# K scores of a one-query attention backward: 16 wide matmuls per head and a 32x32 transpose in place of 64 narrow ones

## The chip, the cores and the metric

The kernel runs on one core of one Trainium2 chip. A core has a matrix engine (TensorE, PE in the profile, which writes its results to a memory called PSUM), a vector engine (VectorE, DVE), a scalar engine (ScalarE, ACT), GpSimd (POOL) and a sync engine (SP) that mostly starts transfers; 16 DMA engines move data between the main memory and the on-chip memory (SBUF, 128 partitions). The metric is the time of one execution on the device in microseconds.

## What is computed

Attention with one query per head, forward and backward: 32 heads, 8192 keys of 128 numbers each, bf16. The outputs are the attention's result and the gradients of q, k and v.

```python
B, H, Sq, Skv, Dh = 1, 32, 1, 8192, 128

def _fwd_reference(q, k, v):
    scale = q.shape[-1] ** -0.5
    scores = jnp.einsum('bhqd,bhkd->bhqk', q, k) * scale
    attn = _softmax(scores, axis=-1)
    return jnp.einsum('bhqk,bhkd->bhqd', attn, v)

def reference(q, k, v, grad_out):
    _out, _vjp = jax.vjp(_fwd_reference, q, k, v)
    return (_out, *_vjp(grad_out))
```

Per head, with p the softmax of the scores s: out = sum of p v; dp = v · grad_out; ds = p (dp - sum of p dp) times the scale; dq = sum of ds k; dk = ds times q, for every key; dv = p times grad_out, for every key. K and V are read once (134 MB), dk and dv written once (134 MB). With one query, each product with K or V is a matrix times a vector, and dk and dv are outer products.

## The kernel before

A head's K, V, dk and dv are tiles of 128 partitions by 64 rows ("slots") by 128 numbers, 2 MB each: partition p holds the keys 64p to 64p + 63. All tiles of a head are processed whole; the loop over heads (line 307) overlaps two of them. In iteration h it does the first half of head h (K scores, softmax, V's part, dv) and the second half of head h - 1, called p_ in the code (the sum of p dp, ds, dk, dq). The order in which instructions are written is the order in which every engine gets them (`manual_schedule`, line 98); each engine works off its own in order and waits where data is missing.

**K scores.** The 128 numbers of a key lie along a partition, but a matmul sums over partitions, so K must be turned. `k_blocks(h, u)` (line 152) does that for a quarter u of the slots (16 of 64): one VectorE transpose of 32x32 blocks, two bf16 numbers taken as one f32 word, from Kt into the quarter u of XK, a tile with one buffer whose quarters are interleaved in memory. After it, partition 32a + j of XK holds word j of the keys of the partitions 32a to 32a + 31. `k_scores(h)` (line 161) then runs 64 matmuls with K as the stationary operand (128 columns) and `q_blk[:, h, c, :]` as the moving one: 4 columns, q's numbers in one quadrant of 32 partitions and zeros elsewhere. The 64 are 16 slots times 4 (2 word blocks times the 2 halves of a word). The scores come out in PSUM tile `s` with the quarter u in the wrong place: `s_mask` (line 171, VectorE) multiplies by `in_quad` and spreads, and `s_swap` (line 179) does 8 passes of small matmuls with `lane` that put the scores in natural rows, `x["sn"]`, partition p with its 64 keys.

**Softmax.** The maximum over the row (`mx`, L339) and over partitions (a TensorE transpose and `nbias`, L350), the exponent on ScalarE from `x["sn"]` (`e`, L355), its sum by a matmul with ones (L356), the reciprocal (`rinv`, L366), p repeated four times (`p_rep`, L368, ScalarE).

**V's part.** `v_transposes` (L198, 32 f32 transposes on TensorE per head, four to a PSUM bank), `v_copy` (L189, ScalarE, PSUM to XV), `v_scores` (L208, 16 matmuls of 512 columns, four of them side by side on quarters of the array) and in the next iteration `v_back` (L215, a VectorE transpose of the PSUM bank; L218). `pd_sum` (L280) sums p dp over partitions on TensorE, `ds_of` (L283: `pdt`, `ds`, `ds_rep`) follows on VectorE. `contract` (L232) makes out and dq in 16 matmuls of 512 columns each.

**Outer products.** `outer(h, which, r)` (L250) makes a quarter of dk or dv on VectorE and starts the store after the last quarter (the first and last head: after every second). dk and dv have two buffers each, K three, V two. The loads `load_k(h+2)` and `load_v(h+2)` and all stores are issued by SP's queue, in the order of the code.

**Row broadcast.** `rows_bc(h)` (line 269), at the head's start, brings q and grad_out of the head to all partitions by one matmul (into columns 256 to 511 of the PSUM tile `s`) and a ScalarE cast to `x["qd"]`; both outer products read it. Every 8 heads `gather_copy` and `gather` (lines 237, 241) take out and dq from their accumulators.

**Prologue.** Two small loads of q (SP's queue) and grad_out (ScalarE's queue) into `rows`, the first loads of K and V, memsets on GpSimd (`do_win`, four `win_...`), `four` (line 117, VectorE copies, L120) and four TensorE transposes that give `q_blk`.

Of the kernel before, what the change touches and what calls it, by code (L numbers as in the profile page):

```python
# [8 lines left out]
ACT = mybir.ActivationFunctionType  # L9
ALU = mybir.AluOpType  # L10
AX = mybir.AxisListType
BF16 = mybir.dt.bfloat16
F32 = mybir.dt.float32
PSUM = bass.MemoryType.PSUM

CH = 16
# [9 lines left out]
def kernel(  # L26
# [37 lines left out]

    NG = NT // 4
    NX = NT // 2
    Kt, Vt, XK, XV, st, acc = {}, {}, {}, {}, {}, {}

    def rows_of(x, h, c, parts):
        L = NT // parts  # L70
# [14 lines left out]
        nc.sync.dma_start(Vt[h][:], rows_of(v, h, 0, 1))  # L85

    rows = consts.tile([H, 2, D], BF16)
    nc.sync.dma_start(rows[:, 0, :], q.rearrange("b h s d -> (b h s) d"))
    nc.scalar.dma_start(rows[:, 1, :], grad_out.rearrange("b h s d -> (b h s) d"))
    load_k(0)  # L90
    load_v(0)
# [14 lines left out]
    for which in ("p", "ds"):  # L106
        wins[which] = []
        for i in range(2):
            w = consts.tile([P, NG, 2 * QD - 4], BF16, name=f"win_{which}{i}")
            nc.gpsimd.memset(w[:], 0.0)  # L110
            wins[which].append(w)
    in_quad = consts.tile([P, NQ], F32)
    nc.vector.reduce_sum(in_quad[:], ident[:].rearrange("p (a i) -> p a i", a=NQ), axis=AX.X)

# [37 lines left out]
    def k_blocks(h, u):  # L152


        if u == 0:
            XK[h] = ktpool.tile([P, CH, NB, NCH, QD], F32, tag="XK", name="XK_sb")
        nc.vector.transpose(XK[h][:, :, :, u, :],  # L157
                            slots(Kt[h], u, NCH).rearrange("p g d -> p (g d)").bitcast(F32).rearrange(
                                "p (g w j) -> p g w j", g=CH, w=NB))

    def k_scores(h):
        x = st[h]
        out = x["s"][:, 0:NT].rearrange("p (a g) -> p g a", a=NQ)
        cols = XK.pop(h).rearrange("p g w u i -> p (g w u i)").bitcast(BF16).rearrange(
            "p (g w ui e) -> p g w e ui", g=CH, w=NB, e=2)
        for g in range(CH):
            for c in range(2 * NB):
                nc.tensor.matmul(out[:, g, :], lhsT=cols[:, g, c // 2, c % 2], rhs=q_blk[:, h, c, :],  # L168
                                 start=(c == 0), stop=(c == 2 * NB - 1), skip_group_check=True)

    def s_mask(h):
        x = st[h]
        x["sm"] = small.tile([P, NQ, NCH, CH], F32, tag="sm", name="sm")
        nc.vector.tensor_tensor(  # L174
            x["sm"][:], x["s"][:, 0:NT].rearrange("p (a g) -> p a g", a=NQ).unsqueeze(2)
            .to_broadcast([P, NQ, NCH, CH]),
            in_quad[:].unsqueeze(1).unsqueeze(3).to_broadcast([P, NQ, NCH, CH]), op=ALU.mult)

    def s_swap(h):

        x = st[h]
        x["sn"] = x["s"][:, 128:128 + NT]
        for a in range(NQ):
            nc.tensor.matmul(x["s"][a * QD:(a + 1) * QD, 128:128 + NT], lhsT=lane[:],  # L184
                             rhs=x["sm"][:, a].rearrange("p u g -> p (u g)"),
                             start=True, stop=True, skip_group_check=True)

    def v_copy(h, c):
        nc.scalar.copy(XV[h][:, c * TB:(c + 1) * TB, :], st[h].pop(("T", c))[:])  # L189
# [60 lines left out]
    def outer(h, which, r):  # L250
        x = st[h]
        if r == 0:
            x[which] = gpool.tile([P, NT, D], BF16, tag=which, name="G_" + which)
        G, dst = x[which], out_2 if which == "dk" else out_3
        rep, row = x["ds"] if which == "dk" else x["p"], x["qd"][:, 0 if which == "dk" else 1, :]
        Q = NT // 4
        nc.vector.tensor_tensor(  # L257
            slots(G, r, 4).rearrange("p n (a b) -> p n a b", b=R),
            slots(rep, r, 4).unsqueeze(2).to_broadcast([P, Q, D // R, R]),
            row.rearrange("p (a b) -> p a b", b=R).unsqueeze(1).to_broadcast([P, Q, D // R, R]),  # L260
            op=ALU.mult)
        parts = 1
        if h == 0 or h == H - 1:
            parts = 2
        if r % (4 // parts) == 4 // parts - 1:
            c = r // (4 // parts)
            nc.sync.dma_start(rows_of(dst, h, c, parts), slots(G, c, parts))

    def rows_bc(h):
        x = st[h]  # L270
        x["s"] = psS.tile([P, 512], F32, tag="s", name="s_ps")
        nc.tensor.matmul(x["s"][:, 256:512], lhsT=ident[0:H, h:h + 1].to_broadcast([H, P]),  # L272
                         rhs=rows[:].rearrange("h a d -> h (a d)"), start=True, stop=True,
                         skip_group_check=True)
        x["qd"] = small.tile([P, 2, D], BF16, tag="qd", name="qd")
        nc.scalar.copy(x["qd"][:].rearrange("p a d -> p (a d)"), x["s"][:, 256:512])  # L276

    def pd_sum(h):
        x = st[h]
# [27 lines left out]
    for h in range(H + 1):  # L307
        p_ = h - 1
        if h < H:
            x = st[h] = {}  # L310
            rows_bc(h)
            for u in range(NCH - 1):
                k_blocks(h, u)
        if h > 0:
            v_back(p_)
            pd_sum(p_)
        if h < H:
            k_blocks(h, NCH - 1)
            k_scores(h)
        if h == 0:  # L320
            do_columns()
        if h > 0:
            ds_of(p_)
            outer(p_, "dk", 0)
            dq_of(p_, 0)
        if h < H:
            s_mask(h)
            s_swap(h)
        if h > 0:
            dq_of(p_, 1)  # L330
            outer(p_, "dk", 1)
            if p_ % ST == ST - 1:
                gather_copy("ds")
                gather(p_, "ds", st[p_]["m"])
        if 0 < h and h + 2 < H:
            load_k(h + 2)
        if h < H:
            mx = small.tile([P, 1], F32, tag="mx")
            nc.vector.reduce_max(mx[:], x["sn"], axis=AX.X)  # L339
            top = small.tile([P, 1], F32, tag="top")  # L340
            nc.vector.tensor_scalar_mul(top[:], mx[:], scale)  # L341
            x["m"] = psM.tile([P, 512], F32, tag="m", name="m_ps")
            nc.tensor.transpose(x["m"][:, 128:256], top[:].to_broadcast([P, P]), ident_f[:])  # L343
        if h > 0:
            outer(p_, "dk", 2)
        if h == 0:
            load_k(2)
        if h < H:
            nbias = small.tile([P, 1], F32, tag="nbias")
            nc.vector.tensor_reduce(nbias[:], x["m"][:, 128:256], axis=AX.X, op=ALU.max, negate=True)  # L350
            v_transposes(h, 0)
            v_transposes(h, 1)
            e = x["e"] = small.tile([P, NT], F32, tag="e", name="e")
            rs = small.tile([P, 1], F32, tag="rs")
            nc.scalar.activation(e[:], x["sn"], ACT.Exp, bias=nbias[:], scale=scale, accum_out=rs[:])  # L355
            nc.tensor.matmul(x["m"][:, 0:1], lhsT=ones_f[:], rhs=rs[:], start=True, stop=True,  # L356
                             skip_group_check=True)
            v_copy(h, 0)
            v_copy(h, 1)
            v_transposes(h, 2)  # L360
        if h > 0:
            outer(p_, "dk", 3)
        if h == H:
            break
        rinv = x["rinv"] = small.tile([P, 1], F32, tag="rinv", name="rinv")
        nc.vector.reciprocal(rinv[:], x["m"][:, 0:1])  # L366
        x["p"] = small.tile([P, NT, R], BF16, tag="prep", name="p_rep")
        nc.scalar.activation(x["p"][:], e[:].unsqueeze(2).to_broadcast([P, NT, R]), ACT.Copy, scale=rinv[:])  # L368
        nc.scalar.copy(window(h, "p")[:, :, QD - 4:QD], x["p"][:, :, 0].rearrange("p (g j) -> p g j", j=4))  # L369
        x["p_s"] = small.tile([P, NT], F32, tag="p_s", name="p_s")  # L370
        nc.vector.tensor_scalar(x["p_s"][:], e[:], rinv[:], scale, op0=ALU.mult, op1=ALU.mult)
        v_copy(h, 2)
        for c in range(3, NX // TB):
            v_transposes(h, c)
            v_copy(h, c)
            if c == 4:
                contract(h, "p")
        if h % ST == ST - 1:
            gather_copy("p")
        v_scores(h)  # L380
# [45 lines left out]
```

## Time and profile before

| what | us |
|---|---|
| median of 3 runs (644.03 to 644.63) | 644.06 |
| the profiled execution, its own time | 644.45 |
| its span, first to last instruction | 642.7 |
| TensorE matmul busy | 404.0 (63%) |
| VectorE busy | 537.9 (84%) |
| ScalarE busy | 194.4 (30%) |
| GpSimd busy | 5.9 (1%) |
| K transposes (L157), 128 of them | 151.4 |
| K score matmuls (L168), 2048 of them | 59.8 |
| mask (L174), 32 of them | 13.6 |
| swap matmuls (L184), 256 of them | 13.7 |

The page reads as follows. Busy time is time in which an engine works on an instruction; the matmuls of TensorE overlap, so their busy time is no measure of use. The page also cuts the span into 40 slices of 16 us and gives for each the busy share of an engine in tenths, the TensorE clock granted, the busy share of the DMA engines and what they moved in GB/s. A group of instructions shows its line, engine, operation, the written and the read tiles, their count, the busy time, the mean length of one in ns, and after the second bar the idle time of its engine just ahead of it with what ended most of that. The mean granted clock of TensorE over the span is 0.732 of full speed; in the records it is 0.50 or 1.00 at any moment. The chain of waits follows back from the last instruction what released each step. The DMA queues moved 269.24 MB at a mean of 419 GB/s, 98.4% of 16 engines' span on one queue.

### The profile page before, as it was taken

How to read it: one execution, taken by the hardware profiler on the slowest of the kernel's cores; microseconds unless marked ns; L12 is line 12 of the kernel's file. 1: busy time of each engine (PE TensorE's matmuls, PEld its weight loads, DVE VectorE, ACT ScalarE, POOL GpSimd, SP SyncE). 2: the span in 40 equal slices, each digit the busy share in tenths (PEclk: the TensorE clock that was granted, in tenths of full speed). 3: DMA queues.
4: the chain of work that ended last, by engine and by line, in shares of the span. 5: the costliest groups of instructions: out<-in, count | busy, mean ns of one | idle time of the engine just before them, and what ended most of it. 6: DMA issues, size and time to landing. Idle time of an engine off the chain costs nothing.

```text
span 642.7 us, 12069 instructions
## 1 busy us (share of the span) xinstructions
PE 404.0 (63%) x5128; PEld 289.2 (45%) x5128; DVE 537.9 (84%) x780; ACT 194.4 (30%) x475; POOL 5.9 (1%) x11
## 2 busy tenths in 40 slices
PE   2766667776755865458675577645687555765571
PEld 1544445455443543346553445433465343553350
DVE  6899999987988789788798888898878988789871
ACT  2333333332233331234232333213332133331240
POOL 3000000000000000000000000000000000000000
PEclk9888887775778666877577876668866678765775
DMA  8999999999999999999999999999999999999995
GB/s 346 410 428 430 424 428 429 427 425 430 428 425 420 423 426 428 429 429 428 429 430 426 429 430 423 433 428 429 430 423 433 426 428 430 429 428 427 429 390 209
DMA packets 19686, 269.24 MB, mean 419 GB/s; under 512 B 2353, under 2 KB 2353, under 8 KB 2865
## 3 DMA queue, kind: packets, MB, share of 16 engines
q1 hardware_dynamic: 19584, 268.47, 98.4%
q8 instruction: 40, 0.66, 0.4%
q14 instruction: 14, 0.11, 0.0%
q10 hardware_dynamic: 48, 0.01, 0.0%
HBM read 134.23 MB, written 134.23 MB: 418 GB/s over the span
## 4 chain that ended last, share of the span: by engine, by line
DMA 70%; DVE 24%; ACT 2%; PE 1%; issue 1%; POOL 0%; DVEq 0%; POOLq 0%
DMA out_dram<-G_dv 70%; DVE G_dv L257 14%; DVE XK_sb L157 4%; DVE G_dk L257 3%; ACT XV_sb L189 1%; DVE dpT L215 1%; DVE four L120 1%; ACT p_rep L368 0%; DVE sm L174 0%; PE acc_ds L232 0%; POOL do_win L104 0%; PE m_ps L246 0%; PE s_ps L168 0%; DVE ds L288 0%; PE T_ps L198 0%
## 5 line engine op out<-in xcount | busy, mean ns | idle before, releaser
L257 DVE TENSOR_TENSOR G_dv<-p_rep,qd 128x2048 bf16<-128x2048 bf16 x128 | 148.2, 1220 | 54.7 <-DMA out_dram<-G_dv 45.5
L198 PE MATMUL T_ps<-ident_f,Vt 128*128 128x128 f32 x1024 | 162.4, 318 | 0.5 <-DMA Vt<-in_v_dram 0.5
L257 DVE TENSOR_TENSOR G_dk<-ds_rep,qd 128x2048 bf16<-128x2048 bf16 x128 | 155.7, 1219 | 1.2 <-DVE ds_rep L292 0.2
L157 DVE STREAM_TRANSPOSE XK_sb<-Kt 128x1024 f32<-128x1024 f32 x128 | 151.4, 1221 | 4.3 <-DMA Kt<-in_k_dram 4.0
L198 PEld LDWEIGHTS T_ps<-ident_f,Vt 128*128 128x128 f32 x1024 | 144.7, 171 | 17.8 <-ACT XV_sb L189 13.6
L189 ACT COPY XV_sb<-T_ps 128x512 f32<-128x512 f32 x256 | 137.0, 590 | 24.0 <-PE T_ps L198 22.8
L280 PE MATMUL m_ps<-pd,ones_f 128*128 128x1 f32 x64 | 18.7, 361 | 162.9 <-DVE prod L218 162.9
L280 PEld LDWEIGHTS m_ps<-pd,ones_f 128*128 128x128 f32 x64 | 16.0, 311 | 168.8 <-DVE prod L218 154.0
L168 PE MATMUL s_ps<-q_blk,XK_sb 128*128 128x4 bf16 x2048 | 59.8, 168 | 22.9 <-DVE pdt L286 17.6
L168 PEld LDWEIGHTS <-XK_sb 128*128 128x128 bf16 x2048 | 57.1, 104 | 25.8 <-DVE pdt L286 20.2
L232 PE MATMUL acc_ds<-Kt,win_ds 128*32 128x512 bf16 x512 | 67.3, 627 | 0.9 <-ACT win_ds L293 0.9
L293 ACT COPY win_ds<-ds 128x64 bf16<-128x64 bf16 x32 | 7.8, 244 | 197.5 <-DVE ds L288 197.5
L355 ACT ACTIVATE e<-s_ps,nbias 128x64 f32<-128x64 f32 x32 | 10.0, 313 | 133.4 <-DVE nbias L350 133.4
L208 PE MATMUL dp_ps<-XV_sb,do_win 128*32 128x512 bf16 x512 | 34.3, 383 | 24.9 <-ACT XV_sb L189 24.9
L232 PE MATMUL acc_p<-Vt,win_p 128*32 128x512 bf16 x512 | 33.5, 382 | 0.0
L208 PEld LDWEIGHTS <-do_win 128*32 128x32 bf16 x512 | 14.2, 94 | 36.3 <-issue 29.7
L276 ACT CAST qd<-s_ps 128x256 bf16<-128x256 f32 x32 | 11.9, 372 | 43.4 <-PE s_ps L272 43.2
L215 DVE STREAM_TRANSPOSE dpT<-dp_ps 128x512 f32<-128x512 f32 x32 | 21.6, 675 | 0.0
L184 PEld LDWEIGHTS s_ps<-sm,lane 128*32 128x32 f32 x256 | 10.4, 151 | 17.6 <-DVE sm L174 16.7
L343 PEld LDWEIGHTS m_ps<-ident_f,top 128*128 128x128 f32 x32 | 5.8, 182 | 27.3 <-DVE top L341 26.3
L174 DVE TENSOR_TENSOR sm<-s_ps,in_quad 128x256 f32<-128x256 f32 x32 | 13.6, 425 | 4.5 <-PE s_ps L168 2.0
L232 PEld LDWEIGHTS <-win_p 128*32 128x32 bf16 x512 | 10.7, 96 | 12.7 <-ACT win_p L369 2.9
(55 smaller groups left out, 224.0 us busy)
## 6 DMA issues: line engine op xcount, KB each, us to landing
Vt<-in_v_dram SPq DMA_DIRECT2D x32, 2048.0 KB, 32.7
Kt<-in_k_dram SPq DMA_DIRECT2D x31, 2048.0 KB, 30.0
out_dram<-G_dv SPq DMA_DIRECT2D x30, 2048.0 KB, 34.8
out_dram<-G_dk SPq DMA_DIRECT2D x30, 2048.0 KB, 32.3
out_dram<-G_dv SPq DMA_DIRECT2D x4, 1024.0 KB, 13.6
out_dram<-G_dk SPq DMA_DIRECT2D x4, 1024.0 KB, 13.0
Kt<-in_k_dram SPq DMA_DIRECT2D x4, 512.0 KB, 5.2
out_dram<-fin_sb SPq DMA_DIRECT2D x2, 8.0 KB, 13.5
```

The lines of the kernel that those rows point to most:

```text
L157: nc.vector.transpose(XK[h][:, :, :, u, :], slots(Kt[h], u, NCH).rearrange("p g d -> p (g d)").bitcast(F32).rearrange("p (g w j) -> p g w ...
L168: nc.tensor.matmul(out[:, g, :], lhsT=cols[:, g, c // 2, c % 2], rhs=q_blk[:, h, c, :], start=(c == 0), stop=(c == 2 * NB - 1), skip_group ...
L174: nc.vector.tensor_tensor(x["sm"][:], x["s"][:, 0:NT].rearrange("p (a g) -> p a g", a=NQ).unsqueeze(2) .to_broadcast([P, NQ, NCH, CH]), in ...
L184: nc.tensor.matmul(x["s"][a * QD:(a + 1) * QD, 128:128 + NT], lhsT=lane[:], rhs=x["sm"][:, a].rearrange("p u g -> p (u g)"), start=True, s ...
L189: nc.scalar.copy(XV[h][:, c * TB:(c + 1) * TB, :], st[h].pop(("T", c))[:])
L198: nc.tensor.transpose(T_ps[:, i, :], words[:, m * P:(m + 1) * P], ident_f[:])
L208: nc.tensor.matmul(out[b * QD:(b + 1) * QD, :], lhsT=do_win[:, h, e2, 2 - 2 * z:2 - 2 * z + QD], rhs=cols[:, z, e2, :, b * QD:(b + 1) * QD ...
L215: nc.vector.transpose(x["dpT"][:].rearrange("p m r -> p (m r)"), x["dp"][:])
L232: nc.tensor.matmul(acc[which][b * QD:(b + 1) * QD, :], lhsT=window(h, which)[:, g, at:at + QD], rhs=X[:, 4 * g:4 * g + 4, :].rearrange("p ...
L257: nc.vector.tensor_tensor(slots(G, r, 4).rearrange("p n (a b) -> p n a b", b=R), slots(rep, r, 4).unsqueeze(2).to_broadcast([P, Q, D // R, ...
L276: nc.scalar.copy(x["qd"][:].rearrange("p a d -> p (a d)"), x["s"][:, 256:512])
L280: nc.tensor.matmul(x["m"][:, 1:2], lhsT=ones_f[:], rhs=x["pd"][:], start=True, stop=True, skip_group_check=True)
```

## The change

The scores' matmuls are turned round. The stationary operand is now q: a window of 128 columns in the new tile `q_win` [128, 4, 160], which is zero but for the columns 6, 38, 70 and 102, where `q_window(h)` (a ScalarE copy) puts the four columns of `q_blk`. The moving operand is a quarter of K, 512 columns (16 slots times 32 keys, two-byte numbers four bytes apart). A window that starts at column 6 - 2u puts quadrant a of quarter u in PSUM row 32a + 2u. So 4 matmuls per quarter, 16 per head, all accumulate in one PSUM bank, with zeros in the rows that aren't theirs. `s_back` turns the bank's 32x32 blocks with one VectorE transpose into `sT` in SBUF, where partition p holds its 64 scores at stride 2; the maximum and the exponent read that view. Mask, swap and their waits go. The matmuls of a quarter are written right after its transpose: those of the first three quarters thus stand ahead of `pd_sum` on TensorE, the last four where all 64 stood.

The row broadcast of head h + 1 moves to the middle of iteration h: its matmul writes into columns 256 to 511 of the PSUM tile `m` after the sum of exponents, its cast and `q_window(h+1)` follow on ScalarE after the second `v_copy`, ahead of `p_rep`. `qd` gets three buffers. For head 0 both are done ahead of the loop. The prologue has two more memsets on GpSimd, and q's load goes from SP's to ScalarE's queue.

```diff
     rows = consts.tile([H, 2, D], BF16)
-    nc.sync.dma_start(rows[:, 0, :], q.rearrange("b h s d -> (b h s) d"))
+    nc.scalar.dma_start(rows[:, 0, :], q.rearrange("b h s d -> (b h s) d"))
...
+    q_win = []
+    for i in range(2):
+        w = consts.tile([P, 2 * NB, P + QD], BF16, name=f"win_q{i}")
+        nc.gpsimd.memset(w[:], 0.0)
+        q_win.append(w)
...
-    def k_scores(h):
+    def q_window(h):
+        nc.scalar.copy(q_win[h % 2][:, :, 2 * NCH - 2:2 * NCH - 2 + P].rearrange("p c (a r) -> p c a r", r=QD)[:, :, :, 0],
+                       q_blk[:, h])
+
+    def k_scores(h, u):
+        if u == 0:
+            st[h]["s"] = psS.tile([P, 512], F32, tag="s", name="s_ps")
+        cols = XK[h].rearrange("p g w u i -> p (g w u i)").bitcast(BF16).rearrange(
+            "p (g w u i e) -> p w u e g i", g=CH, w=NB, u=NCH, e=2)
+        at = 2 * (NCH - 1 - u)
+        for c in range(2 * NB):
+            nc.tensor.matmul(st[h]["s"][:], lhsT=q_win[h % 2][:, c, at:at + P], rhs=cols[:, c // 2, u, c % 2],
+                             start=(u == 0 and c == 0), stop=(u == NCH - 1 and c == 2 * NB - 1),
+                             skip_group_check=True)
+
+    def s_back(h):
         x = st[h]
-        out = x["s"][:, 0:NT].rearrange("p (a g) -> p g a", a=NQ)
...
-        for g in range(CH):
-            for c in range(2 * NB):
-                nc.tensor.matmul(out[:, g, :], lhsT=cols[:, g, c // 2, c % 2], rhs=q_blk[:, h, c, :],
-                                 start=(c == 0), stop=(c == 2 * NB - 1), skip_group_check=True)
...
+        sT = single.tile([P, CH, QD], F32, tag="sT", name="sT")
+        nc.vector.transpose(sT[:].rearrange("p g r -> p (g r)"), x["s"][:])
+        x["sn"] = sT[:, :, 0:2 * NCH:2].rearrange("p g u -> p u g")
...
-    def rows_bc(h):
-        x = st[h]
-        x["s"] = psS.tile([P, 512], F32, tag="s", name="s_ps")
-        nc.tensor.matmul(x["s"][:, 256:512], lhsT=ident[0:H, h:h + 1].to_broadcast([H, P]),
+    def rows_bc(h, bank):
+        nc.tensor.matmul(bank, lhsT=ident[0:H, h:h + 1].to_broadcast([H, P]),
...
-            rows_bc(h)
+            if h == 0:
+                q_window(0)
+                first = psT.tile([P, 512], F32, tag="T", name="first")
+                rows_bc(0, first[:, 256:512])
             for u in range(NCH - 1):
                 k_blocks(h, u)
+                k_scores(h, u)
         if h > 0:
             v_back(p_)
             pd_sum(p_)
         if h < H:
             k_blocks(h, NCH - 1)
-            k_scores(h)
+            k_scores(h, NCH - 1)
...
-            s_mask(h)
-            s_swap(h)
+            s_back(h)
...
-            nc.vector.reduce_max(mx[:], x["sn"], axis=AX.X)
+            nc.vector.tensor_reduce(mx[:], x["sn"], axis=AX.XY, op=ALU.max)
...
             v_copy(h, 0)
             v_copy(h, 1)
+            if h + 1 < H:
+                rows_bc(h + 1, x["m"][:, 256:512])
+                q_window(h + 1)
             v_transposes(h, 2)
```

More of the change, by code (lines that the diff above doesn't have):

```diff
@@ L66 @@
     NX = NT // 2
-    Kt, Vt, XK, XV, st, acc = {}, {}, {}, {}, {}, {}
+    Kt, Vt, XK, XV, st, acc, qd = {}, {}, {}, {}, {}, {}, {}
     def rows_of(x, h, c, parts):
@@ L159, in k_blocks @@
                                 "p (g w j) -> p g w j", g=CH, w=NB))
-    def k_scores(h):
-        x = st[h]
-        out = x["s"][:, 0:NT].rearrange("p (a g) -> p g a", a=NQ)
-        cols = XK.pop(h).rearrange("p g w u i -> p (g w u i)").bitcast(BF16).rearrange(
-            "p (g w ui e) -> p g w e ui", g=CH, w=NB, e=2)
-        for g in range(CH):
-            for c in range(2 * NB):
-                nc.tensor.matmul(out[:, g, :], lhsT=cols[:, g, c // 2, c % 2], rhs=q_blk[:, h, c, :],
-                                 start=(c == 0), stop=(c == 2 * NB - 1), skip_group_check=True)
-    def s_mask(h):
-        x = st[h]
[L173 to L186, printed above, removed]
+    def q_window(h):
[12 more added lines that the diff above has]
+    def s_back(h):
+        x = st[h]
+        sT = single.tile([P, CH, QD], F32, tag="sT", name="sT")
+        nc.vector.transpose(sT[:].rearrange("p g r -> p (g r)"), x["s"][:])
+        x["sn"] = sT[:, :, 0:2 * NCH:2].rearrange("p g u -> p u g")
     def v_copy(h, c):
@@ L254, in outer @@
         G, dst = x[which], out_2 if which == "dk" else out_3
-        rep, row = x["ds"] if which == "dk" else x["p"], x["qd"][:, 0 if which == "dk" else 1, :]
+        rep, row = x["ds"] if which == "dk" else x["p"], qd[h][:, 0 if which == "dk" else 1, :]
         Q = NT // 4
@@ L267, in outer @@
             nc.sync.dma_start(rows_of(dst, h, c, parts), slots(G, c, parts))
-    def rows_bc(h):
-        x = st[h]
-        x["s"] = psS.tile([P, 512], F32, tag="s", name="s_ps")
-        nc.tensor.matmul(x["s"][:, 256:512], lhsT=ident[0:H, h:h + 1].to_broadcast([H, P]),
+    def rows_bc(h, bank):
+        nc.tensor.matmul(bank, lhsT=ident[0:H, h:h + 1].to_broadcast([H, P]),
                          rhs=rows[:].rearrange("h a d -> h (a d)"), start=True, stop=True,
                          skip_group_check=True)
-        x["qd"] = small.tile([P, 2, D], BF16, tag="qd", name="qd")
-        nc.scalar.copy(x["qd"][:].rearrange("p a d -> p (a d)"), x["s"][:, 256:512])
+        qd[h] = small.tile([P, 2, D], BF16, tag="qd", name="qd", bufs=3)
+        nc.scalar.copy(qd[h][:].rearrange("p a d -> p (a d)"), bank)
     def pd_sum(h):
@@ L354 @@
             rs = small.tile([P, 1], F32, tag="rs")
-            nc.scalar.activation(e[:], x["sn"], ACT.Exp, bias=nbias[:], scale=scale, accum_out=rs[:])
+            nc.scalar.activation(e[:].rearrange("p (u g) -> p u g", u=NCH), x["sn"], ACT.Exp, bias=nbias[:], scale=scale, accum_out=rs[:])
             nc.tensor.matmul(x["m"][:, 0:1], lhsT=ones_f[:], rhs=rs[:], start=True, stop=True,
```

## The prediction

> **What bounds the kernel now.** I read the 40 slices first, then the groups with the wait ahead of each, then the chain that ended last, and then single heads in order of time.
>
> ```profile
> span 642.7 us, 12069 instructions
> ...
> DMA  8999999999999999999999999999999999999995
> GB/s 346 410 428 430 424 428 429 427 425 430 428 425 420 423 426 428 429 429 428 429 430 426 429 430 423 433 428 429 430 423 433 426 428 430 429 428 427 429 390 209
> ...
> L257 DVE TENSOR_TENSOR G_dv<-p_rep,qd 128x2048 bf16<-128x2048 bf16 x128 | 148.2, 1220 | 54.7 <-DMA out_dram<-G_dv 45.5
> ```
>
> The 16 DMA engines are full from the second slice to the 38th, at 420 to 433 GB/s. A head moves four tensors of 2.10 MB (K and V in, dk and dv out), 8.39 MB, or 19.6 us at 428 GB/s. DVE, busy 84%, waits 45.5 us for a store of dv to leave its buffer. The chain shows when that begins:
>
> ```profile
> 87.95 4.63 DVE G_dv L257 x4
> ...
> 105.10 4.64 DVE G_dv L257 x4
> ...
> 537.43 4.64 DVE G_dv L257 x4
> 542.07 0.02 issue
> 542.09 34.87 DMA out_dram<-G_dv
> 576.96 0.03 issue
> ```
>
> Up to 105 us a head takes DVE 105.10 - 87.95 = 17.15 us and nothing holds it up. From there the chain is dv stores, two heads in 577.05 - 537.43 = 39.62 us, 19.8 us each. So DVE has about 2.6 us of room per head. It isn't lost at once either: at 400 us the issues add up to 86 transfers of 2.10 MB = 180.4 MB, the slices to 169.4 MB moved, so 11 MB or 25 us of transfers stand in line.
>
> **The change in one head.** One early head, in order of time (start, length, engine; brackets hold the idle time before):
>
> ```profile
> 41.03 3.49 DVE L157 STREAM_TRANSPOSE XK_sb<-Kt 128x1024 f32<-128x1024 f32 x3
> ...
> 44.45 0.67 DVE L215 STREAM_TRANSPOSE dpT<-dp_ps 128x512 f32<-128x512 f32 x1
> ...
> 45.44 0.58 PE L280 MATMUL m_ps<-pd,ones_f 128*128 128x1 f32 x2 [4.08 <-DVE prod L218]
> 46.47 0.12 DVE L286 TENSOR_TENSOR pdt<-m_ps,rinv 128x1 f32<-128x1 f32 x1
> 46.60 1.87 PE L168 MATMUL s_ps<-q_blk,XK_sb 128*128 128x4 bf16 x64 [0.57 <-DVE pdt L286]
> ...
> 48.58 0.42 DVE L174 TENSOR_TENSOR sm<-s_ps,in_quad 128x256 f32<-128x256 f32 x1
> ...
> 53.10 0.51 ACT L368 ACTIVATE p_rep<-e,rinv 128x256 bf16<-128x256 f32 x1
> ...
> 53.64 1.22 DVE L257 TENSOR_TENSOR G_dv<-p_rep,qd 128x2048 bf16<-128x2048 bf16 x1 [0.27 <-ACT p_rep L368]
> ```
>
> DVE: the mask sm (0.42) goes, the transpose of a PSUM bank comes, the form and size of L215 (0.67): **+0.25 us**. The maximum reads 64 values as before (0.22), now strided from SBUF; I leave it at 0, bounds -0.05 and +0.1.
>
> TensorE: 64 small matmuls (1.87) and 8 of the swap (0.43) go, 16 of 512 columns come. No row has one over the whole array. Nearest are the 512-column matmuls on a quarter of it, which run four at a time: four of L232 take 0.40 at clock 1.00 and sixteen 1.05, so each further round costs (1.05 - 0.40) / 3 = 0.22. At clock 0.50 eight take 1.04 and one 0.63, so a round costs 0.41. The strided read costs nothing there: v_scores (L208) reads two-byte values four bytes apart and also needs 1.05 for sixteen. Bounds for four of the new ones: 0.40 (all at once, as the quarters run) to 4 x 0.63 = 2.5 (no overlap, half clock). I take a round each, being nearest in columns: 0.40 + 3 x 0.22 = 1.05 warm, 0.63 + 3 x 0.41 = 1.86 cold.
>
> Twelve of them now stand on TensorE ahead of pd_sum (L280), and pdt on DVE waits for that, with ds, ds_rep and the dk products queued behind it. Blocks end 1.2, 2.4 and 3.5 us after the head's start. Warm, the last four end at 3.5 + 1.05 = 4.55; pd_sum started at 45.44 - 41.03 = 4.41 before, and pdt, which takes 0.70 from there (622.14 to 622.84 at the end of the kernel, where nothing else is in the way), would be ready at 5.25, under the 5.44 at which it ran. So 0. Cold: 1.2 + 0.63 + 11 x 0.41 = 6.35, pdt at 7.05: 1.6 us late. Which one? In this head the clock stayed at 1.00 until 45 us, though TensorE idled from 41.4, and was 0.50 after. The new scores fill that gap from 42.2 on, so I take warm while DVE sets the pace, **0**, and keep 1.6 as the other end. Later, with DVE waiting for stores, the idle time is longer (341.7 to 348.6; the clock fell at 345.7) and a part is cold, but then the 1.6 us lies in the wait of some 2.3 us for the store.
>
> [...]
>
> The last four scores run beside pdt, ds, ds_rep and the first dk product (2.1 us on DVE), so s_back finds them done: 0. That cover holds warm with 1 us to spare, and cold just about.
>
> ACT: the cast of the row broadcast (0.37 alone) and the new q_window (a small copy; the 64-element one of L369 takes 0.25) now stand between v_copy and p_rep, which ends last ahead of dv. Three v_copies of 0.59 take 1.56, so 0.1 of each overlaps: 0.4 to 0.6, I take **+0.5**. The broadcast matmul (0.28) sits behind the sum of exponents on TensorE; rinv waits for dk's last product anyway. Taken from the head's start these two free nothing on DVE.
>
> Sum per head: 0.25 + 0 + 0.5 = **+0.75**, 17.9 us, or 18.2 with the gathers (2.3 us, every eighth head). Store waits cover it; without that cover it would be 31 x 0.75 = 23 us.
>
> **The start and the end.** These are the places where the DMA engines aren't full. First two rows in order of time, then three windows of 1 us (the last number is GB/s, the DMA share stands before it):
>
> ```profile
> 3.34 3.52 DVE L120 COPY four<-rows 32x128 bf16<-32x128 bf16 x4
> ...
> 4.72 1.74 POOL L110 MEMSET win_ds<- 128x960 bf16 x2
> ...
> 26.00:27.00 1.00, 0.00 (x0) 0.00 (x0) 1.00 (x2) 0.08 (x1) 0.00 (x0) 1.00 1.06 377
> 27.00:28.00 1.00, 0.00 (x0) 0.00 (x0) 0.97 (x2) 0.00 (x0) 0.00 (x0) 0.97 0.75 279
> 28.00:29.00 1.00, 0.58 (x2) 0.50 (x2) 1.00 (x3) 0.00 (x0) 0.00 (x0) 0.50 0.88 361
> ```
>
> (1) q's load leaves SP's queue (0.39, from 0.73), so K's first load is issued at 0.73 instead of 1.19: **-0.46**. On ACT's queue it goes first; grad_out's load and the table load come 0.4 later, and their readers start at 7. (2) The first of L120's copies begins at 3.34 and lasts 3.19 us, and the other three pass in 0.3 us when POOL's memsets end at 6.46: DVE is held by POOL. Two more memsets of 640 elements, by the rows of 960 (0.90) and 2176 (1.92) some 0.63 each, hold it **+1.2** longer. (3) Head 0's scores: from the last block to the maximum 15.62 - 12.59 = 3.03 before, then 1.05 + 0.67 + 0.1 = 1.8: **-1.2**. (4) ACT, as above: **+0.5**. The first dv store then goes out about 0.5 later, the opening loads end 0.46 earlier, and the thin stretch between them (26 to 29 us: 0.6 us lost at 429 GB/s) grows by up to 0.96; half of that, as it isn't empty: **+0.5**. At the tail dv of head 31 waits 2.30 us for the store of head 29; 0.75 lies inside: 0, and +0.1 for dk of head 30, issued later into a thin line (380 GB/s from 610 to 615).
>
> [...]
>
> Sum: -0.46 + 0.5 + 0.1 = +0.14 us. The profiled execution took 644.45 with a span of 642.7, so 1.75 lies outside; it stands 0.39 over the median. On the median: 644.06 + 0.14 = **644.2**, own range 643.0 to 645.4. A measurement of this kernel tells no change from one of about 0.2%, or 1.3 us.
>
> **Rivals.** *The clock stays cold and pdt comes late.* For it: after each K phase the clock is at 0.50 for 6 to 10 us. Against: the gap that cooled it is filled. 17.15 + 0.25 + 0.5 + 1.6 + 0.3 (gathers) = 19.8 us a head on DVE. It decides from (621.2 - 24.4) / 31 = 19.25 us on, where 31 heads of DVE alone reach the end of the last dv product (621.2); at 19.8 the end is 31 x 0.55 = 17 us later, 661; half cold, nothing, three quarters cold about 646 to 650. Slower.
>
> *Blocks and scores take turns.* XK's four blocks are interleaved in one tile with one buffer. If the transposes of block u+1 must wait for the matmuls that read block u, DVE loses about 1.05 three times a head: 21.3 us, 24.4 + 31 x 21.3 + 21 = 706. Against: the two touch different bytes. No step of the profile before has this order, so it shows neither.
>
> *A faster start.* If POOL's memsets don't hold DVE longer, the first store goes out 0.7 earlier and the thin stretch is no longer than before: -0.46 - 0.2 to -1.0, 643.4 to 642.6; a warm clock in the last heads' chain could add some tenths. That little is done at all to the time is its neighbour.
>
> **How the numbers follow.** Forecast 0.56 (0.04 faster, 0.46 same, 0.06 slower), cold clock 0.18 (0.02 same, 0.16 slower), taking turns 0.10 (slower), faster start 0.16 (0.12 faster, 0.04 same). Faster 0.16, same 0.52, slower 0.32. The range goes from 642.6 to 653, which leaves out the turns, the worst third of the cold case, and the best of the start.
>
> **What would show it.** Right: DVE still waits for dv stores, by some 1.6 us a head instead of 2.3; pdt follows K's last block without idle time; the DMA line stays at 9. Wrong: idle time of DVE ahead of pdt or between K blocks, slices under 415 GB/s, or no more idle time for stores. [...] A rate of the DMA engines that moves by 0.5% would break the forecast from outside.

## The result, and the profile after

| | before | after |
|---|---|---|
| median, us | 644.12 (8 runs, 643.94 to 644.73) | 642.38 (8 runs, 642.20 to 642.60) |
| the profiled execution: own time / span | 644.45 / 642.7 | 642.33 / 640.5 |
| instructions | 12069 | 8426 |
| TensorE mean granted clock | 0.732 | 0.857 |
| first dv product starts, us | 19.33 | 21.91 |
| VectorE waits for dv stores, us | 45.5 | 28.1 |

The ratio is 0.9971 (95% interval 0.9960 to 0.9982): 1.74 us or 0.3% faster, where 644.2 was forecast, with 642.6 as the lower end. These are the page's lines after the change (span, DMA share and GB/s in 40 slices, a queue's packets, MB and share, the dearest VectorE group):

```profile
span 640.5 us, 8426 instructions
...
DMA  8999999999999999999999999999999999999994
GB/s 353 421 415 427 429 431 426 425 433 426 429 431 427 429 431 427 430 429 429 431 427 432 428 425 437 427 424 436 428 425 435 428 426 434 426 430 433 427 405 193
...
q8 instruction: 26, 0.43, 0.3%
...
L256 DVE TENSOR_TENSOR G_dv<-p_rep,qd 128x2048 bf16<-128x2048 bf16 x128 | 148.2, 1220 | 35.3 <-DMA out_dram<-G_dv 28.1
```

Still the 16 DMA engines are full from the second slice to the 38th, and VectorE still waits for stores, though less. One line of the page before, which the prediction passed over, has changed by a third:

```profile
q8 instruction: 40, 0.66, 0.4%
```

This queue brings no tensor (all 268.47 MB of them are on q1): named "instruction", it is taken here to bring the program's own instructions, in packets of 16 KB, and the count of its packets goes with theirs. It does so through the same 16 DMA engines as loads and stores: while one of its packets is under way, 15.1 packets of the tensors are on average, and 16.1 otherwise (in the kernel before, from 100 to 590 us). One such packet is called a fetch here. There are 40 - 26 = 14 packets fewer, for 12069 - 8426 = 3643 instructions fewer, 260 to a packet. What a fetch costs the kernel is what the experiments ask.

An early head after the change, in order of time (start, length, engine, line, operation, tiles; brackets hold the idle time before):

```profile
112.26 4.63 DVE L256 TENSOR_TENSOR G_dv<-p_rep,qd 128x2048 bf16<-128x2048 bf16 x4 [0.28 <-ACT p_rep L371]
116.80 3.49 DVE L162 STREAM_TRANSPOSE XK_sb<-Kt 128x1024 f32<-128x1024 f32 x3
...
118.85 2.78 PE L177 MATMUL s_ps<-XK_sb,win_q 128*128 128x512 bf16 x12
...
122.24 0.12 DVE L283 TENSOR_TENSOR pdt<-m_ps,rinv 128x1 f32<-128x1 f32 x1
122.37 1.03 PE L177 MATMUL s_ps<-XK_sb,win_q 128*128 128x512 bf16 x4 [0.62 <-DVE pdt L283]
...
124.18 0.71 DVE L184 STREAM_TRANSPOSE sT<-s_ps 128x512 f32<-128x512 f32 x1
...
130.22 4.63 DVE L256 TENSOR_TENSOR G_dv<-p_rep,qd 128x2048 bf16<-128x2048 bf16 x4 [0.29 <-ACT p_rep L371]
```

The head takes VectorE 130.22 - 112.26 = 17.96 us. Four score matmuls take 1.03, the three blocks still end in 3.49, and `pdt` has no idle time ahead of it. The chain of waits shows when store waits and load waits take over from VectorE:

```profile
221.81 4.63 DVE G_dv L256 x4
226.44 3.41 DVE XK_sb L162 x3
239.78 4.63 DVE G_dv L256 x4
244.41 3.41 DVE XK_sb L162 x3
251.94 30.10 DMA Kt<-in_k_dram
282.06 3.50 DVE XK_sb L162 x3
```

Before, the chain went over to stores at 105 us. Now VectorE, slower by 0.8 us a head, leads until 252, and K's loads follow. From there both kernels go at the pace of the transfers; if bytes alone set that pace, little could be won.

### The profile page after: what moved, and what is told of

It reads as the page before. It is cut to its first block, busy times and chain, and to the rows that moved or that the text cites. A ratio compares the mean times of both kernels' runs of the same rounds, so it can differ in the third digit from the quotient of the medians.

```text
span 640.5 us, 8426 instructions
## 1 busy us (share of the span) xinstructions
PE 466.5 (73%) x3336; PEld 276.5 (43%) x3336; DVE 546.7 (85%) x780; ACT 205.5 (32%) x507; POOL 7.1 (1%) x13
## 4 chain that ended last, share of the span: by engine, by line
DMA 45%; DVE 39%; PE 9%; ACT 4%; issue 1%; DVEq 0%; ACTq 0%
DMA Kt<-in_k_dram 45%; DVE XK_sb L162 15%; DVE G_dv L256 9%; DVE G_dk L256 7%; PE s_ps L177 3%; DVE dpT L214 2%; PE T_ps L197 2%; PE acc_ds L231 2%; ACT XV_sb L188 2%; DVE sT L184 1%; ACT p_rep L371 1%; DVE prod L217 1%; DVE ds L285 1%; ACT qd L273 1%; DVE four L125 1%
## 5 line engine op out<-in xcount | busy, mean ns | idle before, releaser
L197 PE MATMUL T_ps<-ident_f,Vt 128*128 128x128 f32 x1024 | 178.0, 339 | 1.0 <-DMA Vt<-in_v_dram 0.4
L256 DVE TENSOR_TENSOR G_dv<-p_rep,qd 128x2048 bf16<-128x2048 bf16 x128 | 148.2, 1220 | 35.3 <-DMA out_dram<-G_dv 28.1
L177 PE MATMUL s_ps<-XK_sb,win_q 128*128 128x512 bf16 x512 | 135.8, 397 | 50.1 <-DVE XK_sb L162 26.3
L177 PEld LDWEIGHTS <-win_q 128*128 128x128 bf16 x512 | 52.7, 105 | 123.8 <-issue 83.2
L355 ACT ACTIVATE e<-sT,nbias 128x64 f32<-128x64 f32 x32 | 13.0, 406 | 138.4 <-DVE nbias L350 138.4
L343 PE MATMUL m_ps<-ident_f,top 128*128 128x128 f32 x32 | 11.0, 342 | 60.3 <-DVE top L341 57.3
L231 PE MATMUL acc_p<-Vt,win_p 128*32 128x512 bf16 x512 | 48.3, 516 | 0.5 <-ACT win_p L372 0.5
L231 PE MATMUL acc_ds<-Kt,win_ds 128*32 128x512 bf16 x512 | 33.5, 382 | 0.9 <-ACT win_ds L290 0.9
L184 DVE STREAM_TRANSPOSE sT<-s_ps 128x512 f32<-128x512 f32 x32 | 22.7, 709 | 3.6 <-PE s_ps L177 3.6
L356 PE MATMUL m_ps<-rs,ones_f 128*128 128x1 f32 x64 | 15.4, 310 | 11.5 <-ACT e L355 11.5
L356 PEld LDWEIGHTS m_ps<-rs,ones_f 128*128 128x128 f32 x64 | 14.0, 272 | 17.8 <-ACT e L355 17.3
```

The lines of the kernel that those rows point to most:

```text
L177: nc.tensor.matmul(st[h]["s"][:], lhsT=q_win[h % 2][:, c, at:at + P], rhs=cols[:, c // 2, u, c % 2], start=(u == 0 and c == 0), stop=(u == ...
L184: nc.vector.transpose(sT[:].rearrange("p g r -> p (g r)"), x["s"][:])
L197: nc.tensor.transpose(T_ps[:, i, :], words[:, m * P:(m + 1) * P], ident_f[:])
L231: nc.tensor.matmul(acc[which][b * QD:(b + 1) * QD, :], lhsT=window(h, which)[:, g, at:at + QD], rhs=X[:, 4 * g:4 * g + 4, :].rearrange("p ...
L256: nc.vector.tensor_tensor(slots(G, r, 4).rearrange("p n (a b) -> p n a b", b=R), slots(rep, r, 4).unsqueeze(2).to_broadcast([P, Q, D // R, ...
L355: nc.scalar.activation(e[:].rearrange("p (u g) -> p u g", u=NCH), x["sn"], ACT.Exp, bias=nbias[:], scale=scale, accum_out=rs[:])
```

## The experiments

Theory: the fetches of instructions take time of the DMA engines, and 14 fewer give the gain. Rivals: TensorE's shorter or warmer work; q's load on ScalarE's queue; VectorE's own time; the start and the end. The kernel before was timed again on the same chip beside each group of experiments (644.02 us for e1 to e4, 644.19 for e5 to e8, 644.09 for e9 to e11); ratios are to that.

**TensorE instructions put back into the changed kernel (e1_narrow56), and TensorE time alone (e2_wide8).** In both the matmuls stand behind dq's second half; their results go to columns that nothing reads.

```diff
+    def fill(bank):
+        for i in range(56):
+            nc.tensor.matmul(bank[:, 32:36], lhsT=ident[:], rhs=do_win[:, 0, 0, 0:4], start=True, stop=True,
+                             skip_group_check=True)
...
             dq_of(p_, 1)
+            fill(st[p_]["m"])
```

e2_wide8 has 8 matmuls of 512 columns in place of the 56.

> The changed kernel with 56 extra 4-column matmuls per head on TensorE (results not used), put after dq where TensorE idles for some 2 us; they add 3584 instructions and so bring the count back to that of the kernel before. Theory fetch (the gain is DMA time that instruction fetches no longer take: 40 fetches of 16 KB before, 26 after, about 1.04 us of one DMA engine each): 14 more fetches, so at least 14 x 1.04 / 16 = 0.9 us of the 1.74 us gain is lost, and all of it if fetches also slow the packets beside them: 643.3 to 644.1. Theory timing (the gain is in the order of work on TensorE and DVE): 642.4, as the matmuls fall into idle time. Theory start (K's first load is issued 0.46 us earlier): 642.4.

> The control for the narrow matmuls: the changed kernel with 8 extra 512-column matmuls per head at the same place (results not used), about 1.8 us of TensorE per head as the 56 narrow ones take, but only 512 instructions or 2 fetches. Theory fetch: 642.4 to 642.6. If it is TensorE's time or clock that counts, it moves as the 56 narrow ones do.

e1: 12003 instructions, 40 fetches, 644.66 us, ratio 1.0009 [1.0000, 1.0017]: the whole gain is gone, and a little more than the theory took. e2: 8899 instructions, 28 fetches, 642.49 us, ratio 0.9973 [0.9963, 0.9984]: the gain is still there, though `pdt` waits 10.1 us for TensorE in e2 and 4.8 us in e1. So it isn't TensorE's time.

**Twice as many (e3_narrow112), and the same 56 in the kernel before (e6_before_narrow56).**

> The changed kernel with 112 extra 4-column matmuls per head (56 after dq, 56 after V's scores, where TensorE idles too; results not used): 28 more fetches than the changed kernel. Theory fetch: twice the effect of 56, 644.2 to 645.8. Theories timing and start: 642.4, unless the matmuls run into the K scores.

> The kernel before with 56 extra 4-column matmuls per head after dq (results not used), so 14 more instruction fetches, 54 in all. Theory fetch: as much slower as the changed kernel became with them, 1.8 to 2.5 us: 645.9 to 646.6, with DMA busy time up by some 1.8 us. If the 2.2 us there came from TensorE's time in the new order of work, this is 644.1, as TensorE idles here for longer.

Both had 54 fetches. e3 took 650.74 us, 1.0103 [1.0090, 1.0117], and e6 651.77 us, 1.0118 [1.0103, 1.0132]; both are longer than expected. They can't be read as fetches alone, as VectorE's waits in e6 show (engine, tile, line, what it waited for: us in total, times, longest):

```profile
DVE nbias L356 <- PE m_ps L349: 40.7, 32, 3.0
```

Before, this wait came to 7.5 us in 4 times. The added matmuls stood ahead of the transpose that `nbias` waits for. In e3 the same happened to `pdt`, 25.4 us. A filling has to be put where the engine is idle and nobody waits behind it.

**Fewer instructions in the kernel before (e9_before_few), and more of them where TensorE is idle (e10_before_narrow56_early).** e9 has 16 score matmuls of 16 columns per head in place of 64 of 4 and leaves out the scores of 12 of every 16 slots; e10 adds 56 matmuls that nothing reads. VectorE's instructions and the transfers of tensors stay as they were.

```diff
-        for g in range(CH):
+        for g in range(0, CH, 4):
             for c in range(2 * NB):
-                nc.tensor.matmul(out[:, g, :], lhsT=cols[:, g, c // 2, c % 2], rhs=q_blk[:, h, c, :],
+                nc.tensor.matmul(out[:, g:g + 4, :], lhsT=cols[:, g, c // 2, c % 2],
+                                 rhs=q_blk[:, h, c, :].unsqueeze(1).to_broadcast([P, 4, NQ]),
                                  start=(c == 0), stop=(c == 2 * NB - 1), skip_group_check=True)
```

```diff
             rows_bc(h)
+            for i in range(56):
+                nc.tensor.matmul(x["s"][:, 64:68], lhsT=ident[:], rhs=q_blk[:, 0, 0, :], start=True, stop=True,
+                                 skip_group_check=True)
```

> The kernel before with 16 score matmuls of 16 moving columns per head in place of 64 of 4; the scores of 12 of every 16 key slots are left out, so the values are not those of the kernel before, while VectorE, ScalarE and every transfer stay as they were. About 1,500 fewer matmuls, 3,000 fewer instructions of TensorE, so some 28 instruction fetches in place of 40. Theory of the fetches (they take time of the 16 DMA engines that loads and stores then lack): 641.9 to 642.8 us, about 1.3 to 2.2 below the kernel before of this call. Rival, that the gain came from something else in the change (q's queue, VectorE's shorter work, K's scores made early): 643.9 to 644.3, as the kernel before.

> The kernel before with 56 matmuls of 4 columns per head added behind the row broadcast at the head's start, where TensorE is idle for some 3.6 us a head until the product of the step before is summed; the results go to 4 columns that nothing reads. Some 54 fetches in place of 40, with no wait of VectorE longer by more than 0.3 us a head. Theory of the fetches: 645.5 to 647.5. Rival, that the earlier 651.8 of such a filling came from VectorE's waits behind it alone: 643.9 to 644.5.

Beside 644.09 us for the kernel before, e9 took 641.77, ratio 0.9965 [0.9953, 0.9978], with none of the change in it. e10 took 647.93, ratio 1.0060 [1.0046, 1.0073]. Both went a little further than the theory's ranges (641.9 and 647.5). From the pages of e9 and then e10:

```profile
span 639.7 us, 8997 instructions
...
q8 instruction: 28, 0.46, 0.3%
```

```profile
span 646.9 us, 15653 instructions
...
q8 instruction: 54, 0.88, 0.5%
```

VectorE's waits for TensorE are nearly those of the kernel before in e10 (`nbias` 7.5 us in both, `rinv` 7.6 against 5.7, `pdt` 0.5 in all). So fewer instructions alone make the kernel faster, and more alone make it slower. Of e9's 2.32 us some 0.24 belong to its start: its first dv product begins at 18.08, 1.25 us earlier, and e7_start below shows that 2.23 us there are worth 0.42. The rest is (2.32 - 0.24) / 12 = 0.17 us for each fetch; e10 gives (647.93 - 644.09) / 14 = 0.27, e1 against the changed kernel (644.66 - 642.38) / 14 = 0.16.

A fetch takes 1.04 us of one DMA engine (the packets' median), 0.065 us if it were spread evenly over 16. Why two to four times as much? Each transfer has 16 reports of landing in the trace, and a wait for it ends with the last: in the kernel before, each of the 19 waits of a dv product for a store ended 0.09 us after the 16th report of that store. If the reports belong to the engines, which the trace doesn't name, the engine that got the most fetches would set the pace; that is the author's estimate. The last dv product in order of time, of the kernel before, of e9 and of e10:

```profile
616.56 4.63 DVE L257 TENSOR_TENSOR G_dv<-p_rep,qd 128x2048 bf16<-128x2048 bf16 x4 [2.30 <-DMA out_dram<-G_dv]
```

```profile
613.60 4.63 DVE L258 TENSOR_TENSOR G_dv<-p_rep,qd 128x2048 bf16<-128x2048 bf16 x4 [2.28 <-DMA out_dram<-G_dv]
```

```profile
620.83 4.63 DVE L257 TENSOR_TENSOR G_dv<-p_rep,qd 128x2048 bf16<-128x2048 bf16 x4 [2.42 <-DMA out_dram<-G_dv]
```

Each waits for a store of dv. In e10 it lands 4.27 us later than before, though by 600 us e10 has moved as many bytes (sums over windows of 20 us: 0.1 us of transfers apart; that counts the fetches, and without them e10 is 0.4 MB or 0.9 us behind). And just then its engines, taken together, aren't full. Two windows of 4 us in the kernel before, then in e10 (the last two numbers are the DMA share and GB/s):

```profile
612.00:616.00 4.00, 4.00 (x29) 3.72 (x32) 1.98 (x5) 3.24 (x9) 0.00 (x0) 0.62 0.90 385
616.00:620.00 4.00, 3.22 (x45) 1.91 (x37) 3.44 (x4) 2.50 (x5) 0.00 (x0) 1.00 0.96 403
```

```profile
612.00:616.00 4.00, 4.00 (x75) 2.31 (x73) 3.85 (x7) 0.00 (x0) 0.00 (x0) 0.50 0.80 340
616.00:620.00 4.00, 4.00 (x38) 3.30 (x36) 2.14 (x5) 3.14 (x9) 0.00 (x0) 0.79 0.78 332
```

With 54 fetches a fifth of the engines' time goes empty, in the second window while VectorE waits for a store: by the author's reading most engines are through with their share, and some aren't.

The trace's records of single packets show how this comes about. From 100 to 590 us, in the kernel before as in e10, 15.1 packets of the tensors are under way on average while a fetch is, and 16.1 otherwise: a fetch takes the place of one engine's packet. In the kernel before, each of the 35 fetches from 60 to 600 us is followed within 0.02 us by a packet of a tensor that takes 0.97 to 1.17 us (median 1.02) where the median of all is 0.61. So a fetch holds up an engine by an estimated 1.04 + 1.02 - 0.61 = 1.45 us, 0.09 us spread evenly over 16. What is left of the 0.16 to 0.27 is put down to unevenness. The time from the first of a transfer's 16 reports to the last grows over the run. Medians for the transfers that land in the first 60 us, and from 540 to 600 us:

| kernel | fetches | first 60 us | 540 to 600 us |
|---|---|---|---|
| e9_before_few | 28 | 1.3 | 8.4 |
| e2_wide8 | 28 | 1.1 | 10.0 |
| after the change | 26 | 0.8 | 10.3 |
| before | 40 | 1.9 | 12.0 |
| e1_narrow56 | 40 | 1.2 | 12.9 |
| e10_before_narrow56_early | 54 | 2.1 | 16.1 |

The reports drift apart, further with more fetches (though not by their number alone: 26 and 28 give 8.4 to 10.3), and a wait ends only with the last. The trace doesn't name the engine of a packet, so which ones carry the fetches stays open, and with it why a fetch cost 0.16 us in one kernel and 0.27 in another.

**q's load back on SP's queue (e4_q_on_sp), and on ScalarE's in the kernel before (e5_before_q_on_act).** Each changes one word of the load of `rows`.

```diff
-    nc.scalar.dma_start(rows[:, 0, :], q.rearrange("b h s d -> (b h s) d"))
+    nc.sync.dma_start(rows[:, 0, :], q.rearrange("b h s d -> (b h s) d"))
```

> The changed kernel with q's small load back on SP's queue, ahead of K's first load. Theory start: K's loads are issued 0.46 us later again, 642.8. Theories fetch and timing: 642.4 or a little less, as q lands sooner (1.7 us after its issue instead of 3.2) but the first copies wait for GpSimd anyway.

> The kernel before with one edit, q's small load on ScalarE's queue instead of ahead of K's loads on SP's. Theory start: K's first load is issued 0.46 us earlier, and the changed kernel with q back on SP's queue lost 0.98 us: 643.1 to 643.6. Theory fetch: the rest of the gain (40 fetches against 26) is not in it.

e4: 643.36 us, ratio 0.9987 [0.9978, 0.9996], which is 0.98 over the changed kernel. e5: 643.72, ratio 0.9992 [0.9984, 1.0001], 0.47 under the kernel before that was timed beside it. Both lie a little above what either theory had (642.8 and 643.6 at most). K's first load is issued at 0.74 instead of 1.19 us. The move helps by some 0.5 to 1 us; e5's interval takes in no effect.

**The start mended (e7_start).** This is the changed kernel's start, in order of time:

```profile
3.95 4.07 DVE L125 COPY four<-rows 32x128 bf16<-32x128 bf16 x4 [0.52 <-DMA rows<-in_q_dram]
...
6.41 1.21 POOL L115 MEMSET win_q<- 128x640 bf16 x2
...
9.31 1.28 ACT L167 ACT_TABLE_LOAD   x1 [9.31 <-DVE q_blk L136]
...
10.91 6.37 PE L177 MATMUL s_ps<-XK_sb,win_q 128*128 128x512 bf16 x16 [2.42 <-ACT win_q L167]
17.32 0.72 DVE L184 STREAM_TRANSPOSE sT<-s_ps 128x512 f32<-128x512 f32 x1 [3.57 <-PE s_ps L177]
...
21.91 4.63 DVE L256 TENSOR_TENSOR G_dv<-p_rep,qd 128x2048 bf16<-128x2048 bf16 x4 [0.28 <-ACT p_rep L371]
```

The copies end at 8.02, just behind GpSimd's memsets (6.41 + 1.21 = 7.62). ScalarE's table load stands ahead of its first copy and waits with it for `q_blk`, so 1.28 us fall on the path that before lay in an idle stretch at 1.19. And 16 matmuls take 6.37 us, 0.40 each. The first of them start 0.43 apart, as score matmuls later in this run do where the granted clock is 0.50 (median 0.43; 0.22 at 1.00); the records of the clock begin at 16.49 us, with 1.00, and from then on the matmuls follow faster. The edit clears the windows on VectorE and puts a tiny ScalarE copy first:

```diff
+    warm = consts.tile([P, 1], F32)
+    nc.scalar.copy(warm[:], ones_f[:, 0:1])
...
-        nc.gpsimd.memset(w[:], 0.0)
+        nc.vector.memset(w[:], 0.0)
         q_win.append(w)
```

> The changed kernel with two edits in the prologue: the two memsets of q_win on VectorE instead of GpSimd, and a tiny ScalarE copy first, so that its table load doesn't wait for q_blk. The first dv product starts some 2.5 to 3 us earlier (21.9 now). Theory DMA (only full transfer time counts): the thin stretch of the DMA engines between the opening loads and the first stores shrinks, 0.2 to 0.8 us: 641.6 to 642.2. If DVE set the pace, the whole 2.5 us would show: 639.9.

It took 641.96 us, ratio 0.9966 [0.9954, 0.9978]. Its start:

```profile
1.01 0.67 DVE L117 MEMSET win_q<- 128x320 uint32 x2
...
1.64 1.28 ACT L104 ACT_TABLE_LOAD   x1 [1.64 <-PEq L415]
...
4.14 2.60 DVE L127 COPY four<-rows 32x128 bf16<-32x128 bf16 x4 [0.71 <-DMA rows<-in_q_dram]
...
9.14 5.92 PE L179 MATMUL s_ps<-XK_sb,win_q 128*128 128x512 bf16 x16 [1.93 <-DVE XK_sb L164]
15.10 0.72 DVE L186 STREAM_TRANSPOSE sT<-s_ps 128x512 f32<-128x512 f32 x1 [2.63 <-PE s_ps L179]
...
19.68 4.63 DVE L258 TENSOR_TENSOR G_dv<-p_rep,qd 128x2048 bf16<-128x2048 bf16 x4 [0.29 <-ACT p_rep L373]
```

The table load is out of the way, and the copies end at 6.74 with the last memset at 6.60. Dv starts 21.91 - 19.68 = 2.23 us earlier, of which 642.38 - 641.96 = 0.42 us reach the end (the intervals overlap, so this size is loose). It has the lowest time of the kernels that compute everything.

**All scores behind the last block (e8_scores_late).**

```diff
                 k_blocks(h, u)
-                k_scores(h, u)
...
-            k_scores(h, NCH - 1)
+            for u in range(NCH):
+                k_scores(h, u)
```

> The changed kernel with all 16 score matmuls of a head after the fourth block's transpose, where the 64 stood (same instructions, other order). DVE then waits for the scores by some 1.5 to 2.5 us a head (16 x 0.22 = 3.5 us, 2.1 of it under pdt to dk). Theory DMA: the room for stores absorbs it, 642.3 to 643.0. If DVE's pace or the early scores made the gain: 31 x 1.5 = 46 us slower at worst, at least back to 644.

It took 679.74 us, ratio 1.0561 [1.0528, 1.0593]: a miss for the theory of the fetches, which had the room for stores absorb the wait (642.3 to 643.0), and within the other one's bounds (644 to 46 us slower). One head, and VectorE's waits:

```profile
114.41 1.24 DVE L162 STREAM_TRANSPOSE XK_sb<-Kt 128x1024 f32<-128x1024 f32 x1
114.99 5.10 PE L177 MATMUL s_ps<-XK_sb,win_q 128*128 128x512 bf16 x16
120.12 0.72 DVE L184 STREAM_TRANSPOSE sT<-s_ps 128x512 f32<-128x512 f32 x1 [2.52 <-PE s_ps L177]
```

```profile
DVE sT L184 <- PE s_ps L177: 80.1, 32, 3.6
```

TensorE sat idle for 2.97 us during the blocks, its weight loads come 0.43 us apart up to 117.94 us, the spacing that goes with a granted clock of 0.50 in the changed kernel, and now 16 matmuls take 5.10 us instead of the 4.2 that 16 at 1.05 for four would. VectorE waits 2.5 us in each head, 17.96 + 2.5 = 20.5 us a head; the prediction put the pace from which VectorE decides at 19.25, and 31 heads at 1.25 more make 39 us, where 37.4 were lost. So what makes the change affordable is the twelve scores made between the blocks. That VectorE can set the pace doesn't make it the cause of the gain: e9 gains with VectorE's work as it was.

**Finer stores at both ends (e11_start_quarters).** On top of e7_start.

```diff
         if h == 0 or h == H - 1:
-            parts = 2
+            parts = 4
```

> The changed kernel with the start mended as in e7_start (q's windows cleared on VectorE, one tiny ScalarE copy ahead of everything), and the stores of the first and the last head in four pieces in place of two. If what is left at the two ends is the wait for the first piece of a store and the landing of the last piece, the first store starts about 1 us earlier and the last piece is half as long: 641.2 to 641.8. If the bytes of the whole run set the end and the ends are covered, or the smaller pieces' packets cost what they save: 641.8 to 642.3.

It took 643.73 us (11 runs, 642.75 to 644.50), ratio 0.9994 [0.9985, 1.0003]: slower than e7_start by more than either theory had it. Smaller pieces at full DMA engines gave nothing back. The 1.8 us lost are in the records of the packets: those of the tensors hold the 16 engines for 632.8 us in e11 and for 631.1 in e7_start; 1.0 of the difference lies in the packets of 4 KB that take the place of those of 8 KB in the first and the last head.

## Why the prediction was wrong

**The step that failed** is the second paragraph of the part on what bounds the kernel: "A head moves four tensors of 2.10 MB ..., 8.39 MB, or 19.6 us at 428 GB/s". The pace in steady state was taken as fixed by the tensors' bytes, and the working asked of each edit only whether it fits under that pace. Of 64 + 8 matmuls that go and 16 that come it counted TensorE's time, which was covered, and not that the instructions themselves come through the bound resource; it put that term at nothing without a word. By e9's price, 14 fetches x 0.17 = 2.4 us; e1 gives 2.3. That is more than the gain of 1.74. The prediction did name "a rate of the DMA engines that moves by 0.5%" as what would break it, though as something from outside; it came from the change, and was in the page as a line of its own.

**(1), K's loads earlier, -0.46:** confirmed in the trace (issued at 0.74, before 1.19), and worth 0.5 to 1 us in the runs.

**(2), the GpSimd memsets, +1.2:** right. `four` ends at 8.02, 1.16 later than before (6.86), and e7_start, with those two memsets gone, ends it at 6.74. In the kernel before the first copy lasted until 6.53, the last memset in the row until 6.46; in the changed kernel it was 7.69 and 7.62, and in e4 and e5 the first matmul that reads `four` starts at 7.74 and 6.59, behind the end of the last memset at 7.60 and 6.46. In e7_start two of these matmuls start from 5.75 on, ahead of the last memset's end at 6.60. Why copies pass there and not in the others isn't shown.

**(3), head 0's scores, -1.2:** wrong in sign. From the last block (9.15 + 4.60 = 13.75) to the start of `sT` are 3.57 us and to its end 4.3, where 1.8 was forecast and 3.03 stood before. Two things were mis-sized: the score matmuls (1.05 for four was worked out from rows at a clock of 1.00; at the start a matmul took 0.40), and the table load of 1.28 us, which the prediction saw only as something 0.4 later. First dv was to be 0.5 later and was 2.58 later. By e7_start this cost some 0.4 us, about the +0.5 put down for the thin stretch; that it didn't show in the sum is luck.

**(4) and the sum per head, +0.75:** right. 17.96 us, forecast 17.9, though one wait sits elsewhere. The prediction had `rinv` wait for dk's last product anyway; it now waits for ScalarE's cast in nearly every head:

```profile
DVE rinv L369 <- ACT qd L273: 24.9, 31, 1.9
```

The new TensorE rows were right as well: 1.03 for four, forecast 1.05, and `pdt` waits for TensorE 2.1 us in the whole run. VectorE lost 17.4 us of store waits (45.5 - 28.1) and no time at the end, as the room of 2.6 us said.

**The tail, +0.1:** not seen. The last dv product starts at 614.45, 2.11 earlier than before, and still behind a store wait of 2.42: it moved with the transfers' pace.

**The rivals.** Turns between blocks and scores: dead, three blocks end in 3.49 as before. The cold clock: it makes no wait, as `pdt` shows; in the early head above it stays at 1.00 (116 to 124 us), now that the idle stretch is filled. (Before the change it fell at 345.4 us, not at 345.7 as the prediction read.) e8_scores_late shows it (5.10 for 16) together with the wait it would have made. The faster start had the right side and nearly the right size (642.6 to 643.4) for the wrong reason: the start is slower, and the gain is everywhere.

The account in whole: -2.4 (fetches, by e9), -0.5 (q's load, e5), +0.4 (start, e7) = -2.5 against -1.74 measured. The 0.8 that is over lies within the intervals of these parts taken together, each about 0.7 us wide on each side; it isn't explained further.

## What to carry to other kernels

Where the DMA engines are the bound, count instructions as well as bytes: the page's row for the queue of instructions says how many fetches there are, and in this kernel each cost 0.16 to 0.27 us, so a few wide matmuls beat many narrow ones here, though TensorE had time to spare. To test such a cause, change the count alone, in a stretch where the engine idles and nobody waits behind it; put elsewhere, a filling measures its own queue (in e6 the wait of `nbias` grew from 7.5 to 40.7 us). And look at the first use of each engine in a changed start: here the table load of 1.28 us moved from an idle stretch at 1.19 us to 9.31, behind the wait for `q_blk` of the copy that it stands ahead of.

## What the runs showed of the hardware that was not expected

- A fetch of 16 KB of instructions takes 1.04 us of a DMA engine, against 0.61 for a packet of 16 KB of tensor data (medians of the packets' durations); the packet of a tensor behind it takes 1.02; and 12 to 14 fetches moved a run of 644 us by 2 to 4 us.
- With more fetches (54, in e10) the end of the run has engines that go empty (share 0.78 at 616 to 620 us) while a store is still awaited, though as many bytes had been moved; the 16 reports of a transfer's landing drift apart, from 2.1 us to 16.1.
- q's load of 8 KB landed 3.2 us after its issue on ScalarE's queue with K's loads issued beside it, 1.7 us on SP's queue ahead of them.
- The first 16 wide matmuls of the run took 0.40 us each, later ones 0.26 (1.03 for four).
